# A fused attention and long-convolution kernel: 24 places of the stored task order are changed

## The chip, the cores and the metric

One core of a Trainium2 chip runs the kernel. The metric is the device time of one execution in microseconds; lower is better. The core's engines work in parallel and each takes its own queue in order: TensorE (PE, matmuls, with its weight loads PEld), VectorE (DVE), ScalarE (ACT), GpSimd (POOL) and SyncE (SP). SP and POOL mostly issue DMA transfers here.

## The reference

There are 8 batches of 3136 rows, 256 columns wide, and two parts that follow each other. The first is an attention without softmax, the second a gated long convolution through the Fourier transform.

```python
scores = (1 / S) * z @ z.T                    # z: 3136 x 64
out    = maximum(scores, 0)**2 @ v            # v: 3136 x 256
x      = u * out
x1, x2, x3 = split(x @ w_proj, 3)             # each 3136 x 256
conv   = irfft(rfft(x2, axis=rows) * rfft(filter, axis=rows))
result = (x1 * conv * x3) @ w_out
```

## The kernel before

**Tiles.** The 3136 rows of a batch are cut into 25 row tiles of up to 128 and, the other way, into 7 chunks of 512, 512, 512, 512, 512, 256 and 320 columns of the score matrix. A *unit* (b, c, k) is the k-th small group of row tiles (two, mostly) of chunk c in batch b.

**A unit's steps.** TensorE makes the scores into a PSUM pair (task kind S). A *relu* copies them into a buffer R (on ACT at line 1956 or on DVE at line 1958), and a *square* writes the bf16 weights into a buffer A (ACT at line 1965, DVE at line 1967). TensorE then multiplies A with v in two halves, called W and V, into the chunk's accumulator. There are 8 buffers A, 3 buffers R and 4 PSUM pairs; scores, accumulators and all later matmuls share the pairs.

**Mirrors.** The score matrix is symmetric. For the next two chunks a unit is not computed again: a DMA transpose on SP's queue (line 1885) writes the transposed A into a *mirror tile*, M_t for the next chunk and M2e_t or M2o_t for the one after, and the units of kind M read it. There is one buffer of each, so a new mirror can be written only when the last reader of the old one is done, and an A buffer that is mirrored comes free only when its transposes have landed.

**After the last unit of a chunk.** DVE multiplies the accumulator with the transposed u (line 2012); two projections and a product (line 1293) make the gates x1·x3; another projection and a first transform (`dft1`) go to a scratch in DRAM, from which the spectrum's matmuls (kind Q, products at line 1394) load it. The result goes to DRAM again, and for each chunk an inverse transform, a product with the gates (line 1499), the output matmul, an eviction to `ost_t` (two buffers) and a store (line 1548) follow. This tail of one batch runs between the units of the next. Inputs are cast on the way in by POOL's DMAs: z (line 662, then a copy that doubles it on DVE, line 1650, and a transpose on SP, line 1657), v (line 688), u (line 662, then a transpose on SP, line 1602). A small copy on POOL (a *tick*, lines 673 and 676) makes such a cast wait for a unit.

**The order.** `Plan.go` does not plan: it reads a stored list. `ORDER` holds two characters for each task, of all engines in one sequence; each task is emitted in that sequence, and so each engine's queue is the subsequence of its own tasks. `ENGINES` says for each of 1426 tasks that could run on either whether ACT or DVE does it. `BANKS` gives the number of the PSUM pair to each of 1054 tasks that take one. A few entries of `ORDER` are *fillers*, matmuls whose result nobody reads.

```python
for k in codes:
    if k >= len(every):
        self.fill(k - len(every))
        continue
    task = every[k]
    ...
    self.run(task, e, start)
```

SP waits inside its queue: a transfer that is not ready holds all behind it. Its DMA issues use eight semaphores in turn.

Of the kernel before, what the change touches and what calls it, by code (L numbers as in the profile page):

```python
# [20 lines left out]
NJ = 16  # L21
# [34 lines left out]
    "r}r~2e3Y2f363ks03i3Z3l2g2u372h2w3as13r3B3ss23vs33w2p3b2i2q3c3m2js42k3t3d3n3e3x3f3C2l0c2v0es50d3Q3y3R"
    "s60f3$0g3D3%3)s73j3*s83&3q3Ss93+3;3p3u3<3#3o3(3z3:3=3!3E3,sA3F494G4AsB3>4H3/0lsCsD4B4I0msE0nsF4N4J4C"
    "4K4OsG0o4R4D3-4S3?4E3G4TsH4P444X4UsI4Y3H3T4F3I4b3U454L4csJ4M4Z4i4W4d4msK4n4j0p4e4V3.0q4Q0r4o4a4f4vsL"
    "4k0s4h4p3J4wsM4l4g4x3K3@3L3V4q4?sN464ssO4@3[sP3]50sQ4t514u4[4y520t57473^4]584^sR0usS0v533_4z4_4{594|"
    "0w4}5D4r3{5M4:5EsT4;4~5NsUsV5FsW565O5h555A5l5i5s5B5C5msX5G545JsY5t5wsZ5j5L5#3M5n5P5x5K3N5usa5o5$sb5y"  # L60
# [2046 lines left out]
```

## Time and profile before

| what | value |
|---|---|
| median of three runs | 946.8 us (941.12, 946.80, 946.83) |
| profiled execution: device time, span | 942.77 us, 940.9 us |
| busy: PE, DVE, ACT, POOL | 97%, 89%, 87%, 26% of the span |
| mean granted TensorE clock | 0.997 |
| moved by DMA | 170.70 MB, 181 GB/s in the mean |

The page gives busy times by engine, the span in 40 slices, the DMA queues, the chain of work that ended last, and groups of instructions by line. Beside it the trace answers for a stretch: busy time by engine, or the instructions in order of time. A line of the latter gives start and length in us, engine, line, operation, output <- input, a count, and in brackets the engine's idle time before it with what ended it. "SPq" is SP's queue; the length of a DMA issue there is that of the issue, not of the transfer.

### The profile page before, as it was taken

The page shows a single profiled execution, that of the slowest core. Times are in us where ns is not written, and L with a number is a line of the kernel's source. Part 1 is how long each engine was busy: PE and PEld are TensorE (multiplying, and loading weights), DVE is VectorE, ACT ScalarE, POOL GpSimd, SP SyncE. Part 2 cuts the span into 40 slices and gives each one's busy share as a digit, 9 for nine tenths or more (in the row PEclk, how much of TensorE's full clock was granted, in tenths as well). Part 3 has the DMA queues.
Part 4 walks back from the last instruction along what each step waited for, and adds up shares of the span by engine and source line. Part 5 has one row for each costly group of instructions (what it writes and reads, how often), then busy time and mean ns, then how long its engine had stood idle before and what let it go on. Part 6 is the DMA issues. An engine that isn't in the chain of part 4 may idle for free.

```text
span 940.9 us, 30306 instructions
## 1 busy us (share of the span) xinstructions
PE 914.0 (97%) x12425; PEld 555.4 (59%) x12425; DVE 838.7 (89%) x1117; ACT 819.6 (87%) x952; POOL 247.6 (26%) x585
## 2 busy tenths in 40 slices
PE   8999999999999999999999999999999999999985
PEld 3445655566554666556565565666565666676654
DVE  8886899999888998999889988999988999899795
ACT  7877898999889998898989999899988999899673
POOL 5143322332332312223122231333123141101030
PEclk9999999999999999999999999999999999999999
DMA  9899899989999789998999989998999979898867
GB/s 158 155 176 163 141 156 197 185 144 173 169 218 201 151 190 168 206 200 146 192 173 212 177 160 189 178 223 149 200 167 208 224 128 202 202 205 140 207 193 232
DMA packets 331644, 170.70 MB, mean 181 GB/s; under 512 B 242887, under 2 KB 307143, under 8 KB 331505
## 3 DMA queue, kind: packets, MB, share of 16 engines
q1 hardware_dynamic: 301624, 131.98, 70.2%
q0 software_dynamic: 29168, 35.13, 25.8%
q8 instruction: 97, 1.59, 0.7%
q10 hardware_dynamic: 712, 1.66, 0.6%
q14 instruction: 43, 0.34, 0.2%
HBM read 90.26 MB, written 53.05 MB: 152 GB/s over the span
## 4 chain that ended last, share of the span: by engine, by line
PE 83%; ACT 5%; DMA 5%; DVE 5%; issue 2%; SPq 0%; POOL 0%; DVEq 0%; ACTq 0%; POOLq 0%
PE ps_s L553 82%; DMA M_t<-A_t 3%; ACT R_t L1956 2%; DVE xh L1394 1%; DVE A_t L1967 1%; DMA zn_t<-in_z_dram 1%; ACT A_t L1965 1%; DVE xT_t L2012 1%; DMA A_t<-spec 0%; ACT xh L619 0%; DMA spec<-uT_t 0%; ACT ost_t L619 0%; ACT s_t L619 0%; DVE gs_t L623 0%; ACT R_t L619 0%
## 5 line engine op out<-in xcount | busy, mean ns | idle before, releaser
L553 PE MATMUL ps_s<-A_t,v_t 64*128 64x512 bf16 (+5 forms) x4766 | 515.7, 352 | 1.1 <-DVE A_t L1967 1.0
L553 PEld LDWEIGHTS <-v_t 64*128 64x128 bf16 (+1 forms) x6528 | 305.8, 98 | 185.9 <-PE ps_s L553 19.2
L1956 ACT ACTIVATE R_t<-ps_s 128x1024 f32<-128x1024 f32 (+3 forms) x359 | 336.8, 961 | 50.4 <-PE ps_s L553 47.2
L1965 ACT ACTIVATE A_t<-R_t 128x1024 bf16<-128x1024 f32 (+2 forms) x281 | 271.8, 992 | 12.0 <-DVE R_t L1958 4.9
L1967 DVE SCALAR_TENSOR_TENSOR A_t<-R_t 128x1024 bf16<-128x1024 f32 (+3 forms) x211 | 233.6, 1123 | 17.6 <-ACT R_t L1956 10.3
L553 PE MATMUL ps_s<-zT_t 64*128 64x512 bf16 (+5 forms) x1186 | 191.4, 352 | 4.4 <-DVE gate_t L1293 1.7
L1958 DVE TENSOR_SCALAR R_t<-ps_s 128x1024 f32<-128x1024 f32 (+4 forms) x153 | 170.3, 1124 | 23.7 <-PE ps_s L553 13.3
L676 POOL COPY tick<-A_t 1x1 bf16<-1x1 bf16 x159 | 54.3, 341 | 426.0 <-ACT A_t L1965 262.0
L553 PE MATMUL ps_s<-xT_t,wp 64*128 64x512 bf16 (+3 forms) x976 | 124.3, 352 | 0.5 <-DVE R_t L1958 0.4
L553 PEld LDWEIGHTS <-zT_t 64*128 64x128 bf16 (+1 forms) x1219 | 68.9, 97 | 52.8 <-issue 9.8
L553 PE MATMUL ps_s<-M_t,v_t 64*128 64x512 bf16 (+4 forms) x860 | 96.6, 353 | 1.8 <-DMA M_t<-A_t 1.7
L619 ACT ACTIVATE x_t<-ps_s 128x1024 bf16<-128x1024 f32 (+3 forms) x75 | 69.4, 927 | 20.9 <-PE ps_s L553 18.1
L1394 DVE TENSOR_TENSOR xh<-xh,H 128x1024 bf16<-128x1024 bf16 x120 | 81.8, 685 | 2.9 <-ACT xh L619 2.0
L1293 DVE TENSOR_TENSOR gate_t<-ps_s,x_t 128x512 bf16<-128x512 f32 (+2 forms) x112 | 64.5, 617 | 12.4 <-PE ps_s L553 10.3
L2012 DVE TENSOR_TENSOR xT_t<-ps_s,uT_t 128x512 bf16<-128x512 f32 (+2 forms) x112 | 64.0, 614 | 6.5 <-PE ps_s L553 6.1
L1499 DVE TENSOR_TENSOR yT_t<-ps_s,gate_t 128x1024 bf16<-128x1024 f32 (+2 forms) x53 | 56.9, 1078 | 12.9 <-PE ps_s L553 11.7
L553 PEld LDWEIGHTS <-wp 64*128 64x128 bf16 (+1 forms) x976 | 47.8, 96 | 30.0 <-PE ps_s L553 2.0
L553 PE MATMUL ps_s<-wp,xT_t 64*128 64x256 bf16 (+2 forms) x944 | 64.0, 266 | 0.1
L553 PE MATMUL ps_s<-wo,yT_t 64*128 64x256 bf16 (+2 forms) x904 | 62.3, 266 | 1.0 <-DVE yT_t L1499 0.5
L662 POOL DMA_DIRECT2D un_t<-in_u_dram x112 | 58.1, 519 | 18.5 <-issue 16.0
L688 POOL DMA_DIRECT2D v_t<-in_v_dram x112 | 58.4, 525 | 13.6 <-issue 10.3
L553 PEld LDWEIGHTS <-xT_t 64*128 64x128 bf16 (+1 forms) x944 | 43.5, 97 | 19.1 <-issue 0.6
(157 smaller groups left out, 910.2 us busy)
## 6 DMA issues: line engine op xcount, KB each, us to landing
out_dram<-ost_t SPq DMA_DIRECT2D x60, 256.0 KB
spec_in_t<-spec SPq DMA_DIRECT2D x56, 192.0 KB
spec<-gs_t SPq DMA_DIRECT2D x56, 192.0 KB
v_t<-in_v_dram POOLq DMA_DIRECT2D x80, 128.0 KB, 4.5
un_t<-in_u_dram POOLq DMA_DIRECT2D x80, 128.0 KB, 4.5
spec<-s_t SPq DMA_DIRECT2D x40, 256.0 KB
conv_in_t<-spec SPq DMA_DIRECT2D x34, 256.0 KB
out_dram<-ost_t SPq DMA_DIRECT2D x18, 128.0 KB
```

Source lines behind the costliest of these rows:

```text
L553: got = nc.tensor.matmul(o, *args, **kw)
L619: got = nc.scalar.activation(out_, in_, AF.Copy)
L662: nc.gpsimd.dma_start(out=t[ds(j * N1, N1), lo - t0 : hi - t0, :], in_=x[:, n2 : n2 + hi - lo, :])
L688: nc.gpsimd.dma_start(out=t[ds(j * N1, N1), ds(v_at(a), (b - a) * D)], in_=r[:, n2 + a - lo : n2 + b - lo, :].rearrange("p t d -> p (t d)"),)
L1293: has_read(nc.vector.tensor_tensor(o[:, :, ::-1] if h == 0 else o, p, x, ALU.mult), p)
L1394: nc.vector.tensor_tensor(x[:, 1 - i], x[:, 0], h, ALU.mult)
L1499: has_read(nc.vector.tensor_tensor(yb["y"][:, :, 0:w], p, gates[b, c][:, :, 0:w], ALU.mult), p)
L1956: has_read(nc.scalar.activation(r, p, AF.Relu), p)
L1958: has_read(nc.vector.tensor_single_scalar(r, p, 0.0, ALU.max), p)
L1965: nc.scalar.activation(a, r, AF.Square, scale=1.0 / float(S))
L1967: nc.vector.scalar_tensor_tensor(a, r, inv_s2, r, ALU.mult, ALU.mult)
L2012: has_read(nc.vector.tensor_tensor(x[:, :, ::-1] if h == 0 else x, f, ut, ALU.mult), f)
```

## The change

No task is added or taken away but one filler (14 in place of 13), and no code changes: the three strings are others. Written out, 462 of some 5,480 tasks stand at another place against the rest of the list, but most of these only trade places with tasks of other engines. On its own engine's queue the order changes for 33 tasks, in these places:

| engine | what moves |
|---|---|
| PE | chunk (0,1): V(0,1,0) goes ahead of score (0,1,9) and the first gate projection of chunk (0,0), and that projection ahead of that score |
| PE | W(0,3,5) three and W(0,3,6) two places back, so that V(0,3,3) and V(0,3,4) come sooner; V(0,3,5) two places back, behind two scores |
| PE | V(0,4,5) two places forward; two of the filter's first transforms three places back |
| PE | V(2,3,2) ahead of W(2,3,5); V(4,2,4) forward and W(4,2,8) back by three; V(5,2,3) and V(5,2,4) three forward, W(5,2,5) four back |
| PE | score (5,4,6) and a projection of chunk (5,1) change places, with two tasks between them |
| PE | among the last tiles a gate projection goes ahead of an output matmul and the inverse transform behind it |
| ACT, DVE | relu (0,1,7) and square (5,3,6) go from DVE to ACT; squares (3,2,8) and (3,2,9) change places; the z copy of line 1650 at 621 us goes behind the eviction that follows it |
| SP | five output stores go back by 4, 8, 7, 6 and 5 places (before, at 281, 300, 395, 541 and 618 us); behind the first come a spectrum load and three mirror transposes, behind the fourth three mirror transposes, two writes of a spectrum and a transpose of u; a spectrum write at 306 us goes back by three |
| SP | transposes of u at 166 and 485 us go back by two and three; a mirror transpose at 274 us goes ahead of a spectrum load; one of the last batch's spectrum loads goes back by three, behind loads for the output of the batch before |
| POOL | at 64 to 70 us a z cast and a v cast go ahead of a tick and the last filter load; a tick at 307 us goes back by four |

`BANKS` follows from the order: 25 tasks take a PSUM pair that another task held before them than was the case. The diff is long; these are its first rows, the rows of the two letters of `ENGINES`, and the first row of `BANKS`:

```diff
 ORDER = (
     "0G0H00010203130I170J1404050K1806150L190716080C1B091G0D1Crx1H0A1A0B1D1L1I1Q0E1M0O1F0F1K1R1N1V1Zry1Wrz"
-    "1S1P1a1c110M1Xr!1d1U1g0N1b1Er#1h1k1Y1er$1l1o1J1ir%1f1p1m1s1j1=1tr&1qr(1>1]1n1u1}1^22r)231r1?1v271_r*"
+    "1S1P1a1c110M1Xr!1d1U1g1E0N1br#1h1k1Y1er$1l1o1ir%1f1J1p1m1s1j1=1tr&1qr(1>1]1n1u1}1^22r)231r1?1v271_r*"
...
 ENGINES = (
-    "aadddddddaaddaaaaaaddaaaddaadaadaadadadadaaaadadaddadddaaaadaadaaddaadaadaaddaddaaaaaaaaadadaddaddad"
+    "aadddddddaaddaaaaaaddaaaddaadaadaadadadadaaaadadaddadddaaaadaadaadaaadaadaaddaddaaaaaaaaadadaddaddad"
...
-    "aaaaaddadaadadadadaaaaddaaadadaaddadadaaaadadaaddadadaaaaaaaddadadaaaddaaddaaaaaadaaaadaaaaaaadadaad"
+    "aaaaaddadaadadadadaaaaddaaadadaaddadadaaaadadaaddadadaaaaaaaddadaaaaaddaaddaaaaaadaaaadaaaaaaadadaad"
...
 BANKS = (
-    "0123012312313213213213212301303103030132132132132321231210210102102123213123121323101201201202303203"
+    "0123012312313213213213212330130130303102102102102021201213213132132120210120121021232032032030131031"
```

More of the change, by code (lines that the diff above doesn't have):

```diff
@@ L56 @@
[L56 to L60, printed above, removed]
@@ new lines @@
+    "r}r~2e3Y2f363ks03i3Z3l2g2u372h2w3as13r3B3ss23vs33w2p3b2i2q3c3m2js42k3t3d3n3e3x3f3C2l0c2v0es50d3Q3Ss6"
+    "0f3$0g3D3%3)s73os83*3ys93&3R3;3p3j3<3q3+3u3#3!3=3(3:3z3E3,493F4G4AsAsB3/4H3>0lsC4B4IsD0msE0nsF4J4K4N"
+    "4C4O0osG4R3-4D4S3?4E3G4TsH4P444X4UsI4Y3H3T4F3I4b3U454L4csJ4M4Z4W4i4d4msK4n4j0p4e4V3.0q4Q0r4o4a4f4vsL"
+    "4k0ssM4p4h4w4g3J4l4x3K3@4s3L3V4q4?sN46sO4@3[sP3]4t50sQ514u4[4y52573^584]sR474^0t0usS530v3_4z4_4{594|"
+    "0w4}5D3{4r5M4:5EsT4;4~5NsUsV5FsW565O5h555A5l5i5s5B5C5m5GsX545JsY5t5wsZ5j5L5#3M5n5K5P5x3N5usa5o5$sb5y"
@@ new lines @@
+    "5H3O5k5)5q5*sc5Q5-3P5%5r5.3|4<5e5&5v5f4=5+3}5(5z3~5<sd485=5I4!se5/5!5>4#sf4$5?5^5p0x0y5,5_5@0z5}sg5:"
+    "5;5{5~5]0!7n7r607osh7vsi7ssjsk7w4%7psl5|5[7t4&7x7z61404(7!sm41sn427%627q7&7u7#437k7)7lso7*7.7(4)7y7/"
+    "7$7?7+4*7@sp4>4+7_7,7-7{7:5R7~5Ssq5T7[sr7;7<807>7|847]0#ss85815U0$5V7^5W0%88827}86st898D8a0&su8E8b83"
+    "7=8f8Asv8F878c8m8Bsw8n8C8g8Gsx8o0(8q8h8d0)sy0*8e8r8i0+sz8j0,8xs!8H8ys#8#8k8s8$8V8l8W0;4,638zs$4-648t"
+    "4.8p8%8u8+s%654/8:8w8,8&8;8v5X8(s&5Y8-665Z5g8[s(8)8<8]8!8|s)8}8^8=9K8*9L8>8/8~9S8.679T8@0-689Ms*0.0/"
@@ new lines @@
+    "8_0<s+0=s,0:5a8{5b8I8X5c0>909U0?5d690@8J9V9Y8K6A9Zs-7m9Ws.0{9N6B9a9O9b91s/8Y9c9P9i9Q9j9F9d9n8?9Gs:9t"
+    "9o9R9u9y9k9e9X9f8L9ps;9z6C8M9v9h9q8N9r6D0[6Es<9w9m9!0]9)A1s=9*A29s9#9$6F0^s>9+0_0|9xs?9g0}0~8O109(A3"
+    "9l8P928Q8ZAB9Hs@A46GA59,ACAF93AGs[AD6TAMs]94s^AH8RANs_9I8SA69-8TAIAQs{A7AR9{958U9|98AOAS9&96A8AX97A9"
+    "AJAY9%99ATs|AU9AAb9J6HAcAA6I9.AZs}AjAE6JAk6M9/6K6jAL6N6LA)AP9:A*s~6RAd6Ot09BAl6SA:AKAe9CAWAft1A;6P6U"
+    "AVt26Q6VAa9Dt3A+Ah6ZA[t46W6at59}9;6XA]Ai6b6c6Y9<6dAm9=6ht6A<t76eA,6iA=A{AnA>A-6zA|A.A^6k6fB2A#A/A$6g"
@@ new lines @@
+    "B69E6lt89~B7t9B36pA?6m6qA@AgA}tAB4BD6nA~9>B06otBBE6r9?B8tCA09@BHA_BFB9BIBQBAB5tDBRB1BJBCBlBvBGA%BmBB"
+    "BwBK6sBLBP6t6x9[A&6ytEBS9]tF6u9^BNB!AoB#tGBntH9_BT6vBxB)BOApBo6wtIB*BqAqB$tJBMB<tKBrB=BUBsB%BtB&C8tL"
+    "C9tM6!B>BiB+BuBj6#BzB,B(CAB-CCtNCJCD6$6(BytO6)CKB;Ar6%tPB/CE6+As6&6,tQCFBpAtAuCLCNtRB:AvCO6-6:AwB?6."
+    "CB6*tS6;6/CSCHtTB@CT6<CPCICUC5B.A(Ax6=CVCXCWAyCYCMAztUC6CbCQ6>CZCgCRChCnCctVCoCaBVCiA!CdCrtWCpEECsCj"
+    "BWCkCeEFBXtXCGBYCfCtEIEGBZEJtYEMCmBaENCqCu6?BbEK6}tZEOtaBcEQClBkB[BdtbERtcB]tdB^teESEUEXEVEHELCvEPEY"
@@ new lines @@
+    "Gut+Fx7NGSt,GTGDGv7OG&GJG(GCGO7PFyGwt-GZG+Fz7cG)GxG<GyC,GWF!t.G=Gat/G,G>GV7QG@7RF-G[t:C^7SGzG-t;F#Gb"
+    "G]G}G.G!G/F.F$G~G^G#GpF/G_G$F%GqGcH0H2GdH3t<GUGeC-G%C.H4t=7LHAC<HBt>C/G*DAH5t?C=C:H6HXC;t@HYC_C>G;C{"
+    "G?C?HeC[H8C@HCt[C]G|HfD0G:t]C|H1D1D3Grt^G{D4C}HlF&C~t_Hm7VF(D57T7WH9F)7XGfHDD6HZ7YD7HpGgHgHnD2t{7Zt|"
+    "HqHht}GhHi7aHaHrHvt~HEHwHsDQHzHbHcH!HxHSGiHTF*HFH#GsH)GjHdH*GtH$HGH%H7u0GkHHH-u1HtH.D8H+HjD9H@HkH[Hu"
+    "DBH/Hou2DCICH]DGH=H:u3H;u4DHIDu5DJH&HyDKDD7dH(HUDEIE7eHVH,7fGlIMu6INDFGmIRH?GnDLu7ISH^IOGou8IXIHH<DM"
@@ new lines @@
+    "ufD$L)LaL*ugD<L-IrL#uhL.DqLxIsL$LyLbL%ItL&I!L>IuuiL+L?LpL]LqIvL(IwL/ujL^JNIxL,M0L@L:JOL_ukDvJPulM1L{"
+    "L;DwL<M5L|umDxM6L=MCunM2MDJQJTM7JRL}L[JSJUD%M8JVK)MEM9M3MHL~MID&LrM4MFD(MJD+JWMBMGMKLsD,JXLcD-JYuoLd"
+    "D_LfLeJZupLgMeDyLhuqMfMmurusMnutD)D=MgMLLiD>MhMoLjMAD?MZMsMaMiMtMjLkMvMkMwE3LtMpMMMuMqM$MNJaM%LlMxuu"
+    "uvMOM*LmuwMyM+JnLnMluxM,M:D.M;M&uyM-M?M.M!MrM<M}M@M#MzM)M~M(D/M[NLD:M/NVuzMbNMM]M>NWu!N0NZu#NNNgMPNa"
+    "M=u$NXMQNONhM^u%LoNPD@MRNbM{JbD[JcNcM|D]MSD;u&NiJdJgN1MTJeJhu(J%JfMdNQMUJoN2u)JpNRNkM_Jiu*NGNlNHNrJq"
@@ new lines @@
+    "JlJjNSNsMcMVJkNTNdNUNtJmJtMWu+JuJru,NvJsMXu-NYNmNeNwJwJ#NfJxNjJ$NnNoN%u.N&JvNqNxN3J&u/JyJ(NyNzN}N(Np"
+    "N4N~NuJzu:N5O5J!N$O6OCJ@J)u;D{O0N)ODu<OGO7J*D|u=MYD}O1N#OHu>O8J+O9OMN6N*ONO2D^N7OEu?NIN]u@N8N^OIJ,NJ"
+    "OQJ-O3OOD~O4OJORE0N!OAOKE1J/OBOSJ:E4J>J.u[J?E5J;J[OTu]OUE6J]u^OXOLJ<u_OYK0J=OFK1J^ObOVOkOcu{OZOPN9J_"
+    "OlE2O(OWJ{NAO)K2u|NKO<u}OdNBN+OaOmK3OhOeOjOfNCK4O=N,OnN_OiO*N-O-u~NDv0O+O>N{NEO[v1O.O]O/OoN.v2v3NFO:"
+    "O^O}O$v4OgO%P7O~N/P8O;P0O_PSO{v5N:PTO@P1PWO?O|P9v6PUE7PXP4PdP6E8PeN;PYv7P5PfE9PhPAPZO,N<PiPmv8EAN=N|"
@@ new lines @@
+    "TNKiKXS;T8TFT9S9KwKjTATLT0TGT1SAQ1vlTOSBTTTYTBSKTHTZKfTCTUTPvmvnTaTISCS<TVSDTbTSS%TcSETeTQS=TfvoS>vp"
+    "TjTgS?TkSFTXS@TRTrTlS[T;vqTdTsTmTiT<TnTWvrTtTqT2T{U0Q2T|U1vsT=vtQ3KkT}TuT>QET?KlQ4Q7KmvuQ8vvThKpU7vw"
+    "Q5U8KqT@TvT[U9QUUBvxKrT,T]UCT-Q6S]T^Q9S^UDTpU2vyT4T_S_UEUIUFQAUMvzUJT3U3QBS{U4T~UNS|UKQCv!S}QFv#QGTo"
+    "QDU6UUv$UVQKQHKnTwUAQLQIKsTxQJS~UOKtQNTyUHU5KuULUPUQUWv%QOUrv&UsT.UyUGQSQPUTUzKxv(QQQTUXQRKyTzUtKzQV"
+    "QMT!v)QWT#U(v*U)v+QkQXT$U!QaUYT%UuQbT:U#UvQYU$T/UZT&QZUmUwUnQdUaU*QeUSv,UbUxU,QfU<URU-v-QgU@U=U%QhU&"
@@ new lines @@
+    "YRQ)Q@YawHVSQ/YTYWYdQ*YeQ:YbQ+YXwIQ;Q,YYYiwJQ~YjYfYmV+Q-wKYnV,YkYcYhYgYoYrV-Y;wLY<YswMYlY@Y=YqYtY}Yp"
+    "Q<wNY[Q=YuY~Q>YSV.wOY]V/Z2V:V[wPZ0Y>Z3Y^Q?Y_Y?Y{YvZ9Y|ZAQ[wQZ4Q]Y,ZDZBY-R7V;wRV<Q^wSZEwTZ5Z1V=Z6Z7ZF"
+    "Z8ZKZCZLWhV>ZGWnZHWiZIWoZMWjWkwUWpWlZPWmX}ZJZQwVZWYwZXZRZbZNZOZcwWY.ZSZTQ_ZYYxY/Q{ZyYyQ|wXZZwYZVZzZd"
+    "Z)WqwZZ*Q}WrZ/WsZaZ!ZeZ+Z#WtZ:Z<Z$waZ=Z,Z;Z%Z-wbZUZ>wcZfZ&Z^wdZ?Z_Z~ZtZ(Zua0wea5Z{aAa6YzZ@wfa1aBwgY!"
+    "Z[R0aCa2Y#Z.a3Z]aIZ|Z}aDa7aJR1afaEwhR2a4aKa8a9apagaHaqatwiaLauaha!aGR3wjara#aiR4ajR8wkRFR5ZvwlR9a&av"
@@ new lines @@
+    "RARNwmaka(WuwnawalaMa$Y$a.woW*a/Y%aaabwpY&ama)Zwa<ana=a_Y(aoa{aFa:Y)bIwqY*a|Zgwra>bJY:axZhwsa*a+ZiY+"
+    "bPasbQa?ayZja@bKZmZkazZlbWwtbXZna,WvZoZxbRa%wuWwacbSW!bTa-W#RBWxadwvbaWya;bbWzRCW_W+W$RDZpa^W,Zqa}Zr"
+    "bga]wwW%W(bhW&aNwxbYW)bLR6aObiW-bMbNbcaPa[W:wyW.bdwzW;beW/W=w!a~W>bOZsbkw#REblW?W]bDbUbEaQW^W@RGbVW<"
+    "W[bmRHaRRIW{w$aSW|bnbZbobrw%XBbsW}bvX1w&W~bww(X0b&btbfbjX2bqb(X4bubxRJX5w)bpb|RKb)w*b}bybzX9w+X3RLX6"
+    "w,XAb~c7b%cCb*c8b#c2X7c0c3cDw-X8cIw.b$cJbFw/w:b+c9c4c5cRaTcEb!cKw;b^cmb_w<cSaUcncFcLc6aeaVcAcBcTcHcq"
@@ L156 @@
[L156 to L160 removed]
+    "Xacffqcgfzfuf&chXbd8f+f#f:Xdcid9f;Xef,dAxIf-XsxJXff?dEf@f(dFf<xKdGf|f!dBf}f/dCXgf[dDerg2f.Xhg3f~f>f]"
@@ new lines @@
+    "f^XlxLXifcgPf=xMg4f{XmgXgQX!xNgYxOfdxPXng1gZgddHxQgRgeg0gadIfNgbg5dJfOgfXodKfPxRXpxSf_XqgSg6gggTghgU"
+    "XjgngKxTgLgogsXtgVXrgtXuxUXvX#gixVX+gygpgWgzgjgkX$xWguX=fQX%gcdLg%gvfRgwg!g&fTxXgmfSg(glg.fUg/grg)fV"
+    "fexYg*gqh6gxh7XwfWg$g:fXh8g-XxgMfYg7h9hAxZXyg8dYhGxag9hHxbhKg#g;hLhIhRgAxchSfZgBgNhVhMgCxdgDhWxehNhT"
+    "hOgEg,dMgFgOg<hBhCdNg+hchDhdh1hXdRh2xfhEdSdOgGdZgHXzhYdPdaxghZdQhghFgIdodThJhQdbhhxhdUhohexidVg=h/hp"
+    "dcgJxjddhUh:hPhiX&g>hqh@X(g?hahjh[xkhkxlh;X)hbX,dWh]h3hmX-xmX.h}dXhfh^h~h_hndeh4g@dfhri2g[i0hli3xng]"
@@ new lines @@
+    "i8dhi9xodgxpi4xqdidmi5hsh<i6dnd&h=iCh>iAdjh)iJh*dpiKh?X*iDh{h|dqdkX/xrdlX:iEdxdrg^xsX;dyiFxtiGiLX<g_"
+    "dsiNg{h5dudtxui7i1dvdziWiBiOiXiId$dwxvd!d%xwd#iMiriPd(iHisxxxyd-iYd)iQiViTiRxzd.h+i#X>d*iZh,itx!i$i)"
+    "X?x#i*d+iug|x$X@i%g}iUhtiaiwg~hux%ixhvd,i/h0ioi]x&ipiyi:iSizi+i!i^hwi;jEi,hxi-jFx(i<x)hyi_jIi(i&i.iv"
+    "jJi[jGjPd:hzjQi?d;i{jKh!jRx*i@h.d<h#jTjLi=d?x+jUx,d@d=x-jYjdx.d>jZjeh$jHi|h%jVjNh&jOjBjajhjmjCjSjijW"
+    "jXjfjnh(jtjbibjcd/jjjujxx/joicjyjgidk{jpx:jvjMjkl0i>k|x;jzx<d[h-l1jqjll4x=d]k}x>jsiel5d^l8x?l9jwl2x@"
@@ L161 @@
+    "qRqhrlqaqjqiqbrqqkrrqoqcqdqlqqqprsqmqnrmmVqsrtqrmWrnrumYmXk;mZrvk<may?mky<y?y<k=y?n#n&n$qtk>n%q%n(k?"
+    "q:n=n)q_k@y>r5y<y>y<rFy>k[quo]rPqvqwy=q&o^q(o_o{q)q;qxq<qyq=q*qzo|q+q!p6o}q>q,q$q#r6pvq-r7q?r8q/q.py"
+    "q@pwpzq[pxrwr9q]q^rGrAp!rHrBrIq{rCrQq|rRrDrEq}rJrSrKq~rLrMrTr0rUrOr2r1rWrVr4rNrXr3"
 )
 ENGINES = (
-    "aadddddddaaddaaaaaaddaaaddaadaadaadadadadaaaadadaddadddaaaadaadaaddaadaadaaddaddaaaaaaaaadadaddaddad"
+    "aadddddddaaddaaaaaaddaaaddaadaadaadadadadaaaadadaddadddaaaadaadaadaaadaadaaddaddaaaaaaaaadadaddaddad"
```

153 lines of the change are left out of this document (47 added, 106 removed).

## The prediction

> **What bounds the kernel now.** I read the page first, then the busy time by stretches, and then the idle times of TensorE one by one. The page:
>
> ```profile
> span 940.9 us, 30306 instructions
> PE 914.0 (97%) x12425; PEld 555.4 (59%) x12425; DVE 838.7 (89%) x1117; ACT 819.6 (87%) x952; POOL 247.6 (26%) x585
> PE 83%; ACT 5%; DMA 5%; DVE 5%; issue 2%; SPq 0%; POOL 0%; DVEq 0%; ACTq 0%; POOLq 0%
> ```
>
> TensorE is busy for 914.0 of 940.9 us and carries 83% of the chain that ended last. No matmul is removed or added but one filler, so a new order can only win what is idle: 26.9 us. The stretches (columns: length, busy PE, weight loads, DVE, ACT, POOL, granted clock, DMA share, GB/s) say where that lies:
>
> ```profile
> 50.00:280.00 230.00, 228.64 (x2900) 130.44 (x2898) 203.00 (x254) 200.99 (x228) 70.97 (x165) 1.00 1.02 172
> 280.00:300.00 20.00, 18.32 (x245) 9.69 (x235) 16.62 (x27) 18.34 (x22) 6.10 (x14) 1.00 1.11 216
> 300.00:540.00 240.00, 236.80 (x3314) 146.52 (x3310) 219.36 (x289) 217.25 (x248) 61.48 (x149) 1.00 1.00 182
> 540.00:560.00 20.00, 19.35 (x288) 13.49 (x285) 17.98 (x24) 17.96 (x25) 6.58 (x17) 1.00 0.92 159
> 560.00:850.00 290.00, 289.43 (x4022) 185.26 (x4020) 266.02 (x341) 266.06 (x299) 67.00 (x160) 1.00 0.99 189
> ```
>
> From 50 to 850 us TensorE is idle for 1.36 + 1.68 + 3.20 + 0.65 + 0.57 = 7.46 us. The other 19.4 us lie before 50 and behind 850, where the change has one place at the start and a few at the end. Also 560 to 850, with 0.57 us in 290, holds several of the changed places; nothing can be won there. So the ceiling of the whole change is about 7.5 us plus a little at the ends, 0.8% and some.
>
> **The largest term: the store that goes behind three mirror transposes.** Around 293 us TensorE has one of its longest idle times.
>
> ```profile
> 280.95 2.28 SPq L1548 DMA_DIRECT2D out_dram<-ost_t  x2
> ...
> 287.90 2.65 SPq L1885 DMA_TRANSPOSE M_t<-A_t  x2
> ```
> ```profile
> 290.64 0.42 DVE L1399 TENSOR_TENSOR xh<-xh 128x512 bf16<-128x512 bf16 x1
> 292.84 1.23 DVE L1967 SCALAR_TENSOR_TENSOR A_t<-R_t 128x1024 bf16<-128x1024 f32 x1 [1.78 <-ACT ost_t L619]
> 293.98 1.28 DVE L1293 TENSOR_TENSOR gate_t<-ps_s,x_t 128x512 bf16<-128x512 f32 x2
> ```
> ```profile
> 295.31 0.39 PE L553 MATMUL ps_s<-zT_t 64*128 64x512 bf16 x2 [1.69 <-DVE gate_t L1293]
> ```
>
> Read from the end. The score matmul at 295.31 waits 1.69 us for the PSUM pair that the gate product (L1293) reads. That product waits behind the square at 292.84, and VectorE stood idle for 1.78 us before the square. The named releaser, an output copy on ScalarE, gives the square nothing: it needs its own relu and a free A buffer, and A buffers are released when their transpose into a mirror tile has landed. The first transpose of the pair at 287.90 reads such a buffer, so I take its landing, at about 292.8, to be what ended the wait; this is inferred, not named by the view. In the new order the store at 280.95, two issues and 2.28 us of SP's queue, goes behind a spectrum load and three transposes, the two at 287.90 among them. Their squares and the last readers of their mirror tile stand several units earlier in the order, so I take them to be ready and held by the queue alone: they move forward by 2.28 us, the square's 1.78 us of idle time goes, and with it the score's 1.69 us. What is late next is the work right behind the score, which waits for nothing in this trace. Term: −1.69 us, with bounds 0 and −1.69. The store itself has one more output tile to spare in its two-buffer pool; if that cover were gone it would cost at most its own 2.28 us of queue.
>
> Here the DMA share is 1.11 in the row 280 to 300 above: the engines that move the bytes are full too. The Trainium skill, "DMA: Bandwidth & Descriptors", section "Issuing engines are not separate DMA queues", says that transfers issued from Scalar, Sync and GpSimd all run on the same 16 DMA engines and interleave. By that rule an earlier issue need not mean an earlier landing, and this term would be 0 in place of −1.69; it is the first rival below.
>
> **The same edit at 541 us.** A store (two issues, 1.18 us) goes behind three transposes, an input transpose and two spectrum writes.
>
> ```profile
> 541.09 1.18 SPq L1548 DMA_DIRECT2D out_dram<-ost_t  x2
> 542.37 6.08 SPq L1885 DMA_TRANSPOSE M_t<-A_t  x3
> ```
> ```profile
> 549.09 0.47 ACT L1965 ACTIVATE A_t<-R_t 128x320 bf16<-128x320 f32 x1 [0.94 <-DMA M_t<-A_t]
> ...
> 551.05 1.37 ACT L1965 ACTIVATE A_t<-R_t 128x640 bf16<-128x640 f32 x2 [0.31 <-DMA M_t<-A_t]
> ```
> ```profile
> 550.20 0.39 PE L553 MATMUL ps_s<-x_t,T 64*128 64x512 bf16 x2 [0.49 <-ACT R_t L1956]
> ...
> 553.06 0.39 PE L553 MATMUL ps_s<-zT_t 64*128 64x512 bf16 x2 [0.16 <-ACT R_t L1956]
> ```
>
> Here the view names the DMA: ScalarE's squares wait 0.94 and 0.31 us for the landing of a transpose, and TensorE then waits 0.49 and 0.16 us for the relus behind them. The transposes come 542.37 − 541.09 = 1.28 us sooner, more than 0.94. Term: −0.65 us, bounds 0 and −0.65.
>
> **The mirror at 80 us.** Two weighing halves that read the old mirror tile (V of units (0,3,3) and (0,3,4)) go ahead of W of (0,3,5) and (0,3,6).
>
> ```profile
> 66.98 0.59 PE L553 MATMUL ps_s<-M_t,v_t 64*128 64x512 bf16 x4
> ...
> 67.84 0.60 PE L553 MATMUL ps_s<-M_t,v_t 64*128 64x512 bf16 x4
> ...
> 79.92 0.60 PE L553 MATMUL ps_s<-M_t,v_t 64*128 64x512 bf16 x4 [0.91 <-DMA M_t<-A_t]
> ```
> ```profile
> 68.52 4.31 SPq L1885 DMA_TRANSPOSE M_t<-A_t  x2
> ```
>
> The matmuls at 67.84 are the last readers of the mirror tile; they end at 68.44, and SP's transposes start at 68.52. In the new order they take the place of those at 66.98, 0.86 us sooner. TensorE later waits 0.91 us for the second of these transposes, so the term is −0.86 us; the bounds are 0 and −0.91, since the casts that POOL moves forward at the same place share the DMA engines. On POOL a z cast and a v cast pass a tick and a filter load; the load's first reader is one of the filter's last transforms, dozens of tasks on, so it is priced at 0.
>
> **The start.** Relu (0,1,7) goes from VectorE to ScalarE and three matmul groups change places.
>
> ```profile
> 29.25 0.76 PE L553 MATMUL ps_s<-zT_t 64*128 64x512 bf16 x4 [1.12 <-DVE xT_t L2012]
> 30.38 0.61 PE L553 MATMUL ps_s<-xT_t,wp 64*128 64x512 bf16 x4 [0.37 <-DVE R_t L1958]
> ```
> ```profile
> 27.91 1.28 DVE L2012 TENSOR_TENSOR xT_t<-ps_s,uT_t 128x512 bf16<-128x512 f32 x2
> 29.11 1.22 DVE L1958 TENSOR_SCALAR R_t<-ps_s 128x1024 f32<-128x1024 f32 x1
> ```
> ```profile
> 28.54 1.02 ACT L1956 ACTIVATE R_t<-ps_s 128x1024 f32<-128x1024 f32 x1
> ```
>
> Before, the score waited for the product that ended at 29.19 and the projection for the relu that ended at 30.33. Now the score (0,1,8) takes the pair that this relu frees. On ScalarE the relu takes the place at 28.54 and ends at about 29.56, so the score starts at 29.60, 0.35 us later than now. Behind it stand a weighing half (0.43 us a group of four: 66.98 and 67.84 are two groups apart), the projection, the other score and the projection's second half, none of which waits: 29.60 + 0.22 + 0.43 + 0.43 + 0.22 = 30.90, where it starts now at 30.38 + 2 × 0.43 = 31.24. Term: −0.34 us. Against it stands 1.02 us more for ScalarE: relu (0,1,6) and the squares of (0,1,4) and (0,1,7) queue behind the new relu, and if TensorE waits for one of them up to 1.02 comes back. Bounds −0.34 and +0.68; I take −0.34, as by the order four weighing groups that need none of these stand first.
>
> **The end, and what is priced at nothing.**
>
> ```profile
> 928.59 0.61 PE L553 MATMUL ps_s<-wo,yT_t 64*128 64x256 bf16 x8 [0.29 <-DVE yT_t L1499]
> ```
>
> Among the last tiles a projection goes ahead of an output group, and the group that feeds the product before 928.59 starts about 0.2 us sooner: −0.2, bounds 0 and −0.29. The other three stores moved back, the squares (3,2,8) and (3,2,9) that change places, the square (5,3,6) that goes to ScalarE, the z copy, and the weighing halves in batches 2, 4 and 5 lie where TensorE waits for none of their kind: batch 5's places lie in 560 to 850, with its 0.57 us of idle time. Their cover is a TensorE queue that is full; without it each would be worth its own instruction, about a microsecond. The loads put a few places later have their consumers many tasks behind them. All these get 0; the bounds are −0.65 (the smaller of the two stores' terms, once more) and +1.02 (one more relu in ScalarE's queue).
>
> **The sum:** −1.69 − 0.65 − 0.86 − 0.34 − 0.2 = −3.74 us. Against the profiled execution's own 942.77 us (its span of 940.9 and 1.9 around it) that is 939.0; against the median of 946.8 it is 943.1. The runs shown are 941.12, 946.80 and 946.83, and with the profiled one their mean is 944.4; less 3.7 it gives 940.7, and I forecast 941 us. 5.7 us of scatter between runs is more than the term itself. One per cent is 9.5 us, about what a measurement of this kernel can tell from no change.
>
> **The rivals.** *The landings do not move, or the list changes less than it seems* (0.35). Most differing characters of the list are tasks of different engines that trade places between each other, which alters no queue; 33 tasks change their order on their own engine. And the DMA share of 1.11 at the main place says that the transposes may land when bytes get through, not when they are issued. For it: that share. Against it: at 541 the share of the stretch is 0.92, and there the named wait is a landing. Only 0 to 1 us is then won (the start and the end): 943.4 to 944.4 from the mean, 941 to 947 by the runs. The skill's rule above speaks for this one.
>
> *Slower: the stores come back* (0.10). Five stores now stand later in SP's queue, among a spectrum's writes and loads. If each blocks SP there and a load behind it becomes what TensorE waits for, the price is their issue time: 2.28 us for the one shown, 1.18 for the other, and the three others, of two issues each, lie between those: 7.0 to 10.3 us in all with no gain. I take 7.0, since the stretch of the larger has the higher DMA share: 942.77 + 7.0 = 949.8 from the profile, 953.8 from the median. It decides from the point where the loads behind a store have less than its 1.18 to 2.28 us to spare. Against it: stores leave the queue's place that the transposes wait for, and nothing in the trace waits for an output store. Only beyond 956.3 is it over 1%: 0.03.
>
> **How the numbers follow.** Forecast 0.55, with its own range 941.12 − 3.74 = 937.4 to 946.83 − 3.74 = 943.1; no gain 0.35; slower 0.10. The range 936.5 to 947.5 holds the first two by the scatter of the runs, and leaves out most of the third and the tails. Faster by over 1% means below 937.3, which needs the whole sum and the fast end of the scatter: 0.09. Slower by over 1%: 0.03. Within: 0.88.
>
> **What would show it.** In the new profile VectorE's idle time before the square near 291 us should be under 0.3 us and the score's 1.69 us gone; ScalarE should not wait for a DMA near 548; the mirror's wait near 79 should be about 0.1 us; near 29 the gate projection should start before the second score. TensorE's idle time from 50 to 850 should be about 4.3 us where it is 7.46. If it is still 7 us or the idle time has only moved on to another place, the second case holds. If TensorE waits for spectrum or conv loads that it did not wait for, the third.

## The result and the profile after

The changed kernel takes 950.94 us in the median of 14 runs (947.14 to 955.90), the kernel before 942.62 us (14 runs, 936.90 to 950.74). The ratio is 1.0077, with a 95% interval of 1.0052 to 1.0102: slower by 0.8%, where 941 us and a small gain were forecast. The ratios here and below leave disturbed runs out, the medians do not. The profiled execution took 955.24 us, 12.5 more than that of before.

The page of the changed kernel, the lines that answer to those of before:

```profile
span 953.5 us, 30308 instructions
PE 918.9 (96%) x12427; PEld 556.0 (58%) x12427; DVE 837.0 (88%) x1115; ACT 819.9 (86%) x954; POOL 246.7 (26%) x585
PE 77%; DMA 9%; DVE 6%; ACT 5%; issue 2%; SPq 0%; DVEq 0%; POOL 0%; ACTq 0%; POOLq 0%
```

TensorE is busy 4.9 us longer with the same matmuls (and one filler more), and idle 7.7 us longer: 34.6 in place of 26.9. DMA has gone from 5% to 9% of the chain. The busy time by stretches of the changed kernel (columns as in the prediction) says where:

```profile
50.00:78.00 28.00, 28.00 (x274) 13.15 (x270) 23.44 (x35) 18.13 (x21) 9.14 (x23) 1.00 1.17 153
78.00:94.00 16.00, 11.32 (x89) 4.70 (x87) 6.86 (x9) 8.03 (x9) 4.15 (x10) 0.79 1.26 168
94.00:280.00 186.00, 185.57 (x2462) 109.20 (x2460) 167.00 (x206) 166.95 (x191) 53.97 (x126) 1.00 0.98 164
280.00:292.00 12.00, 9.31 (x110) 4.95 (x108) 6.72 (x8) 8.81 (x10) 3.72 (x10) 0.86 1.11 192
```

Two stretches stand out, 78 to 94 and 280 to 292. Both have idle time, and in both the granted clock is below 1. The same first stretch before had 155 matmuls where there are now 89:

```profile
78.00:94.00 16.00, 15.00 (x155) 8.79 (x153) 9.97 (x13) 12.89 (x14) 6.56 (x14) 1.00 1.22 171
```

**Near 79 us.** TensorE's order of time in the changed kernel:

```profile
83.16 1.03 PE L553 MATMUL ps_s<-M_t,v_t 64*128 64x512 bf16 x4 [4.58 <-DMA M_t<-A_t]
...
84.42 1.06 PE L553 MATMUL ps_s<-A_t,v_t 64*128 64x512 bf16 x4
...
92.42 0.59 PE L553 MATMUL ps_s<-A_t,v_t 64*128 64x512 bf16 x4
```
```profile
80.50:83.20 2.70, 0.04 (x2) 0.04 (x4) 0.00 (x0) 0.63 (x1) 1.57 (x4) 0.76 1.30 123
83.20:88.00 4.80, 4.80 (x24) 1.71 (x26) 1.23 (x1) 2.43 (x3) 0.77 (x3) 0.50 1.21 165
```

The first row is the group that started at 79.92 us before, after 0.91 us of waiting for its mirror tile. It now waits 4.58 us, and then the clock is halved: a group of four takes 1.06 us in place of 0.59. Matched task by task, TensorE was 0.43 us ahead of before when it came to this place; the waiting group starts 3.2 us late, and at 94 us TensorE is 6.2 us late. So the longer wait costs 3.7 us, and the halved clock behind it nearly all of the other 3. From there to 274 us the distance stays at 6.2 us.

**Near 281 us** come another 4 us, 10.4 in all at 292: a square waits for a mirror's landing, TensorE waits for the relu behind it, and the clock halves again.

```profile
281.77 1.06 ACT L1965 ACTIVATE A_t<-R_t 128x1024 bf16<-128x1024 f32 x1 [3.48 <-DMA M_t<-A_t]
```
```profile
283.79 1.04 PE L553 MATMUL ps_s<-wp,xT_t 64*128 64x256 bf16 x8 [2.69 <-ACT R_t L1956]
```

From 50 to 850 us TensorE is idle for 13.5 us, where 4.3 had been forecast. A smaller loss of 3 us lies between 640 and 750 us, where the prediction saw nothing to win; no experiment was made for it.

**At the first place the diff touches POOL and TensorE**, 12 to 16 us earlier. POOL's queue before and, in the second fence, after:

```profile
64.88 1.23 POOL L762 DMA_DIRECT2D xh<-in_moe_filter_fft_dram  x2 [0.29 <-issue]
...
67.64 1.58 POOL L662 DMA_DIRECT2D zn_t<-in_z_dram  x3
69.17 0.57 POOL L688 DMA_DIRECT2D v_t<-in_v_dram  x1
```
```profile
64.43 1.55 POOL L662 DMA_DIRECT2D zn_t<-in_z_dram  x3 [0.73 <-issue]
65.94 0.56 POOL L688 DMA_DIRECT2D v_t<-in_v_dram  x1
...
66.57 1.23 POOL L762 DMA_DIRECT2D xh<-in_moe_filter_fft_dram  x2
```

The filter load is issued 1.7 us later. The mirror transposes (68.52 us and 4.31 us for the two before) are issued sooner, and their issues hold SP's queue for much longer:

```profile
67.22 7.44 SPq L1885 DMA_TRANSPOSE M_t<-A_t  x2
74.72 3.85 SPq L1885 DMA_TRANSPOSE M2o_t<-A_t  x1
```

The view of the DMA issues gives, as its last number, the time from issue to landing of the two large transfers of the filter load, before and after:

```profile
xh<-in_moe_filter_fft_dram POOLq DMA_DIRECT2D x2, 256.0 KB, 5.6
```
```profile
xh<-in_moe_filter_fft_dram POOLq DMA_DIRECT2D x2, 256.0 KB, 8.5
```

By these rows load and transposes now stand in each other's way. That is the theory which the experiments start from.

### The profile page after: what moved, and what is told of

The parts are those of the page before. It is cut to its first block, busy times and chain, and to the rows that moved or that the text cites. A ratio compares the mean times of both kernels' runs of the same rounds, so it can differ in the third digit from the quotient of the medians.

```text
span 953.5 us, 30308 instructions
## 1 busy us (share of the span) xinstructions
PE 918.9 (96%) x12427; PEld 556.0 (58%) x12427; DVE 837.0 (88%) x1115; ACT 819.9 (86%) x954; POOL 246.7 (26%) x585
## 4 chain that ended last, share of the span: by engine, by line
PE 77%; DMA 9%; DVE 6%; ACT 5%; issue 2%; SPq 0%; DVEq 0%; POOL 0%; ACTq 0%; POOLq 0%
PE ps_s L553 77%; DMA M_t<-A_t 5%; ACT R_t L1956 2%; DVE xh L1394 1%; DMA M2e_t<-A_t 1%; DVE A_t L1967 1%; DMA spec<-gs_t 1%; ACT A_t L1965 1%; DMA v_t<-spec 1%; DMA A_t<-spec 1%; DVE xT_t L2012 1%; ACT xh L619 1%; DMA spec<-s_t 0%; DVE yT_t L1499 0%; DVE xh L1399 0%
## 5 line engine op out<-in xcount | busy, mean ns | idle before, releaser
L1956 ACT ACTIVATE R_t<-ps_s 128x1024 f32<-128x1024 f32 (+4 forms) x360 | 337.3, 962 | 50.2 <-PE ps_s L553 42.5
L1965 ACT ACTIVATE A_t<-R_t 128x1024 bf16<-128x1024 f32 (+3 forms) x282 | 272.7, 993 | 20.6 <-DMA M_t<-A_t 11.0
L1967 DVE SCALAR_TENSOR_TENSOR A_t<-R_t 128x1024 bf16<-128x1024 f32 (+4 forms) x210 | 232.4, 1123 | 25.4 <-ACT R_t L1956 11.3
L1958 DVE TENSOR_SCALAR R_t<-ps_s 128x1024 f32<-128x1024 f32 (+2 forms) x152 | 169.0, 1123 | 25.3 <-PE ps_s L553 15.4
```

The costliest lines, as they stand in the source:

```text
L1956: has_read(nc.scalar.activation(r, p, AF.Relu), p)
L1958: has_read(nc.vector.tensor_single_scalar(r, p, 0.0, ALU.max), p)
L1965: nc.scalar.activation(a, r, AF.Square, scale=1.0 / float(S))
L1967: nc.vector.scalar_tensor_tensor(a, r, inv_s2, r, ALU.mult, ALU.mult)
```

## The experiments

The experiments were timed beside the kernel before on the same chip, in five rounds. "Wait" is TensorE's wait for the mirror near 79 us in the one profiled execution of each; before, it is 0.91 us.

| kernel | median, us | ratio to before, 95% interval | wait, us |
|---|---|---|---|
| changed | 950.94 | 1.0077 [1.0052, 1.0102] | 4.58 |
| changed, stretch at 64 us as before | 944.26 | 1.0014 [0.9982, 1.0046] | 0.15 |
| before, with that stretch as changed | 949.53 | 1.0061 [1.0033, 1.0090] | 2.88 |
| before, POOL's part of it alone | 950.30 | 1.0044 [1.0008, 1.0079] | 2.29 |
| before, TensorE's part of it alone | 946.90 | 1.0032 [0.9998, 1.0066] | 1.67 |
| changed, filter load late | 951.33 | 1.0075 [1.0039, 1.0112] | none; 2.55 at 93 |
| before, casts ahead and load late | 952.96 | 1.0095 [1.0058, 1.0133] | none; 9.37 at 93 |
| before, load early | 944.44 | 1.0001 [0.9965, 1.0036] | none |
| changed, load early | 947.92 | 1.0031 [0.9995, 1.0066] | none |
| changed, 14 fillers ahead of the wait | 951.27 | 1.0102 [1.0068, 1.0136] | 1.48 |
| before, SP's places alone | 942.95 | 1.0005 [0.9969, 1.0040] | none |
| before, other places of PE, ACT and DVE | 944.31 | 0.9995 [0.9961, 1.0029] | none |

### Is it the stretch at 64 us?

Diffs of the list are written as the order of tasks on a queue. The changed kernel, put back there:

```diff
 POOL
-z cast, v cast, tick (0,3,8), filter load
+tick (0,3,8), filter load, z cast, v cast
 PE
-V(0,3,2) V(0,3,3) V(0,3,4) S(0,3,11) W(0,3,5) W(0,3,6) W(0,3,7)
+V(0,3,2) W(0,3,5) V(0,3,3) W(0,3,6) V(0,3,4) S(0,3,11) W(0,3,7)
```

> The changed kernel with one stretch of the list put back to the order of before: the one near 64 to 70 us, which holds POOL's two casts and the weighing halves V and W of chunk (0,3). Everything else is as changed. Theory A (this stretch makes TensorE wait 4.58 us near 79 us and run at a granted clock of 0.50 for about 7 us after it): the wait goes back to about 0.9 us, the clock stays at 1.00 from 78 to 90, and the time falls by about 6 us from the 950.9 of the changed kernel, to 944 to 946, within 0.4% of before. Theory C (the wait is an accident of the one profiled execution, and the 8 us are spread over the other places): no fall, 950 to 952, 0.8% over before.

The opposite edit on the kernel before:

> The kernel before with this one stretch alone changed (POOL's two casts ahead of the filter load, and V of (0,3,3) and (0,3,4) ahead of W of (0,3,5) and (0,3,6)). Theory A: TensorE waits about 4 us for a mirror near 79 us, the granted clock falls to 0.5 behind it, and the time is about 6 us (0.6%) over before, near 948.6. Theory C: within 1 us of before, near 942, the wait near 79 us 0.1 to 0.9 us.

Measured: 1.0014 without the stretch, 1.0061 with it alone. TensorE in the first of the two:

```profile
78.86 0.61 PE L553 MATMUL ps_s<-M_t,v_t 64*128 64x512 bf16 x4 [0.15 <-DMA M_t<-A_t]
```

Theory A holds in both directions, theory C falls. Some 0.6 of the 0.77% are this stretch. Two things did not come as expected: the second kernel waits 2.88 us and not about 4, and behind that wait the clock stayed at 1.00.

### POOL's part or TensorE's?

Each part of the diff above was put alone into the kernel before.

> The kernel before with only POOL's queue changed in this stretch: the z cast and the v cast go ahead of the tick and the filter load; TensorE's order is that of before. Theory A1 (the later filter load is what the mirror transposes meet on the DMA engines): wait near 79 us of 3 to 5 us, 5 to 6 us (0.6%) over before. Theory A2 (it is TensorE's order, which lets the transposes be issued 1.3 us sooner, into the casts): no change, within 1 us of before. Theory A3 (only the two together do it): no change either, so the next kernel decides between A2 and A3.

> The kernel before with only TensorE's order changed in this stretch: V of (0,3,3) and (0,3,4) ahead of W of (0,3,5) and (0,3,6); POOL's queue is that of before. Theory A1: the mirror's wait near 79 us falls from 0.91 us to about 0.1 us, as the prediction's term has it, and the time is 0 to 0.9 us under before. Theory A2: wait of 3 to 5 us, 5 to 6 us over before. Theory A3: no change.

POOL alone: 1.0044, a wait of 2.29 us and a halved clock behind it (three rows of the stretches, then TensorE's row):

```profile
82.00:83.00 1.00, 1.00 (x8) 0.41 (x6) 0.68 (x1) 0.71 (x1) 0.00 (x0) 0.61 1.10 201
83.00:84.00 1.00, 1.00 (x8) 0.33 (x6) 0.00 (x0) 0.97 (x2) 0.00 (x0) 0.50 1.13 290
84.00:85.00 1.00, 1.00 (x8) 0.45 (x6) 0.00 (x0) 0.40 (x1) 0.20 (x2) 0.50 1.31 244
```
```profile
81.38 0.60 PE L553 MATMUL ps_s<-M_t,v_t 64*128 64x512 bf16 x4 [2.29 <-DMA M_t<-A_t]
```

TensorE alone: 1.0032, with an interval that touches no change. Its transposes are issued at 67.34 us, 1.2 us sooner than before, and the wait is 1.67 us, longer and not 0.1 us as the prediction had it. No theory was right alone: A1 saw POOL's part, with a wait shorter than it said, but its gain from TensorE's order did not come. Which part is the larger the two times cannot tell, as their intervals overlap. Both edits push transposes and load into one another, one by a later load, one by earlier transposes.

### Is it the load? Two other places for it

Late first, behind eight tasks of POOL's queue (the expectation counts 12), in the changed kernel and then in the kernel before with the casts ahead:

```diff
 POOL
-... filter load, u cast, tick, tick, v casts, u cast, tick, tick, z cast
+... u cast, tick, tick, v casts, u cast, tick, tick, z cast, filter load
```

> The changed kernel with one task moved: the last filter load on POOL (four transfers, two of 256 KB) goes 12 places back in POOL's queue, behind the z cast near 80 us, so that it is issued when the mirror transposes of 67 to 75 us have landed; its first reader stands near 106 us. Theory A (load and transposes share the DMA engines, and the transposes land late by that): the 4.58 us wait near 79 us falls under 0.5 us, the clock stays at 1.00 there, and the time falls by 6 us or more from 950.9, to 942 to 945. Theory D (the casts or the earlier issue of the transposes do it, not the load): the wait stays over 2 us and the time over 948.

> The kernel before with only POOL's queue changed: the two casts go ahead as in the kernel where POOL alone was changed (0.44% over before), but the filter load goes behind the z cast near 80 us. Theory A: the wait near 79 us is under 0.5 us (0.91 us before, 2.29 us with POOL's queue changed as in the diff), and the time is 0 to 0.9 us under before. Theory D: the wait stays over 2 us and the time 0.4% over before.

The wait at 79 us is gone in both, and the two mirror transposes, at 67.20 and 68.41 us, issue in 2.65 and 2.66 us. The two casts are still issued as early (64 to 66 us), so it is not they alone that delay the mirror. But the time has not moved (1.0075 and 1.0095). SP and TensorE in the first of the two:

```profile
67.20 2.65 SPq L1885 DMA_TRANSPOSE M_t<-A_t  x2
...
84.26 3.61 SPq L1885 DMA_TRANSPOSE M_t<-A_t  x1
```
```profile
95.46 1.04 PE L553 MATMUL ps_s<-M_t,v_t 64*128 64x256 bf16 x8 [2.55 <-DMA M_t<-A_t]
```

and TensorE in the second:

```profile
102.37 1.03 PE L553 MATMUL ps_s<-M_t,v_t 64*128 64x256 bf16 x8 [9.37 <-DMA M_t<-A_t]
```

The load, issued at 80 to 83 us, meets the next mirror transposes at 84 us. The mechanism of theory A holds, its times do not: the load costs where it meets transposes, and here it met others. So a much earlier place was tried. This needs one edit of the code, since the load waits for the tick of chunk 2:

```diff
-filt_ld[c].deps = [(tick_, None)]
-tick_.kids.append(filt_ld[c])
+first = tick_ if c == 0 else first
+t = first if c == 2 else tick_
+filt_ld[c].deps = [(t, None)]
+t.kids.append(filt_ld[c])
```

> The kernel before with the last filter load alone moved forward, behind the two u casts near 31 us (it waits for the tick of chunk 0 in place of that of chunk 2, and stands some ten places earlier on POOL); a stretch from 42 to 45 us in which the DMA engines are nearly idle (share 0.06) lies behind it. Theory A (the load costs where it meets mirror transposes): no wait near 79 us (0.91 us before) nor near 93 us (2.55 and 9.37 us with the load put late), unless the load meets transposes of 30 to 42 us; time 0 to 2 us under before. Theory E (mirror transposes near 80 to 93 us are late anyway, whatever the load does): a wait of 2 us or more near 79 or 93 us, time 3 us or more over before.

> The changed kernel with the same move of the filter load. Theory A: the 4.58 us wait near 79 us is gone and none near 93 us takes its place; the time falls from 950.9 to 942 to 945. If the places outside that stretch are worth the 2.9 us that the prediction gave them, it goes under 941; if they are worth nothing, as the run without the stretch has it, it stays near 943. Theory E: 948 or more, with a wait near 79 or 93 us.

The waits near 79 and 93 us are gone in both. The changed kernel falls from 1.0077 to 1.0031, with intervals that still overlap; the kernel before stays where it was. Transposes at 67 us in the changed kernel:

```profile
67.32 2.90 SPq L1885 DMA_TRANSPOSE M_t<-A_t  x2
```

Theory E falls. But the new place is not free of transposes: those of the mirror near 35 us meet the load, and their issue is stretched. Before and, in the second fence, in the changed kernel with the load early:

```profile
35.84 2.62 SPq L1885 DMA_TRANSPOSE M_t<-A_t  x2
```
```profile
35.50 5.11 SPq L1885 DMA_TRANSPOSE M_t<-A_t  x2
```

TensorE is nevertheless busy for all of the 12 us from 34 to 46 us in both kernels. So the load costs where it meets transposes that TensorE soon waits for, and not with every transpose. The 947.92 us are above the 942 to 945 expected, but the interval reaches from 0.9995 to 1.0066 and holds 944; in this kernel's profiled execution the second loss is still there (a wait of 2.64 us at 276 us, with a halved clock). No version tried is measurably faster than the kernel before.

### What does the halved clock cost?

```diff
 PE
+14 fillers
 W(0,4,3)
```

> The changed kernel with 14 fillers (28 matmuls whose result nobody reads, about 3 us) on TensorE right ahead of the weighing half that waits 4.58 us near 79 us. The mirror lands when it lands; only TensorE is busy for most of the wait. If the clock is what the idle time costs beside its own length: idle time there falls to about 1.6 us, the granted clock stays at 1.00 from 80 to 90 us, and the time is 2 to 2.5 us under the changed kernel, 948.5 to 949. If the halved clock behind the wait costs nothing (other engines would have held TensorE): 951, as changed. Where the wait is shorter than 3 us in a run, the fillers cost the difference.

The clock stayed at 1.00 and the idle time at 1.48 us, as expected, and the time stayed at 951.27. TensorE, then ScalarE, then SP, in that kernel:

```profile
82.42 0.61 PE L554 MATMUL ps_s<-M_t,v_t 64*128 64x512 bf16 x4 [1.48 <-DMA M_t<-A_t]
91.04 0.61 PE L554 MATMUL ps_s<-A_t,v_t 64*128 64x512 bf16 x4 [1.92 <-ACT A_t L1966]
```
```profile
89.02 1.02 ACT L620 ACTIVATE s_t<-ps_s 128x1024 bf16<-128x1024 f32 x1 [2.66 <-DMA specf<-s_t]
```
```profile
77.99 0.57 SPq L1066 DMA_DIRECT2D specf<-s_t  x1
```

Against the changed kernel TensorE gained 2.7 us from 82 to 87 us, which is the clock, and gave 2.1 of it back at 89 us, where ScalarE waited for the landing of a spectrum write that was issued at 77.99 us, behind the transposes on SP's queue. So in this execution the halved clock was real, but most of it lay in the shadow of the same late landings.

### The other places

> The kernel before with SP's places alone: four of the five output stores, the spectrum write and loads, the transposes of u and the mirror near 274 us as changed (with the tick near 307 us, which goes with them); TensorE's order and the stretch at 64 us are those of before. By the prediction's two terms for the stores: 2.3 us under before, with the waits of 1.69 us near 294, 0.81 near 537 and 0.49 near 550 gone. By its rival (the stores come back): 5 to 8 us over before. By what the run without the stretch at 64 us suggests (all other places together 1.3 us over before, with a new wait of 1.5 us near 274): 0 to 2 us over before, the old waits gone and a wait near 274 in their place.

> The kernel before with the changed places of TensorE, ScalarE and VectorE outside the stretch at 64 us and outside SP's places (one store at 618 us goes with them). By the prediction: 0.34 us at the start and 0.2 us at the end are won, the others nothing: 942, within 1 us of before. If these places hold what the run without the stretch had over before: 944, with a wait of TensorE that is not in the trace of before near one of them.

Both are at no change. The prediction's 2.3 us for SP's places (0.9975) lie inside the first one's interval, so the size is not refuted; its rival of 5 us or more is. Near 294 us, with SP's places alone:

```profile
286.92 4.11 SPq L1885 DMA_TRANSPOSE M_t<-A_t  x2
```
```profile
293.37 1.23 DVE L1967 SCALAR_TENSOR_TENSOR A_t<-R_t 128x1024 bf16<-128x1024 f32 x1 [2.46 <-DMA M_t<-A_t]
```
```profile
295.85 0.39 PE L553 MATMUL ps_s<-zT_t 64*128 64x512 bf16 x2 [2.61 <-DVE gate_t L1293]
```

The transposes were issued 1 us sooner than before (287.90), their issue took 4.11 in place of 2.65 us, and the square came 0.5 us later. The wait that should have gone grew to 2.61 us.

The second loss of the profiled execution, near 281 us, is not tied to the diff: the same wait of TensorE for that relu is in the traces of the changed kernel and of four experiments (1.48 to 3.13 us), two of which have SP's and TensorE's orders of before, and in none of the other eight kernels. What makes it come and go was not settled.

## Why the prediction was wrong

- **The ceiling** was right as far as it went: an order can win only idle time. It was taken for the whole question. A new order can also make idle time, and that side had only the stores and about a microsecond for a relu in it.
- **"The load's first reader is dozens of tasks on, so it is priced at 0"** is the step that failed. Nobody waits for the load; but it shares the DMA engines with transfers that somebody waits for. POOL's edit alone measured +0.44%.
- **The mirror at 80 us, −0.86 us.** The transposes were issued 1.3 us sooner, as said; they landed 3 us later, and the term came out at about +6 us with clock and POOL's edit together. The prediction saw that the casts share the engines, and let this only cancel the gain: the bound ended at 0 where it had to reach above. Nor is the 0.91 us wait fixed: the two kernels of "The other places", which keep this stretch as before, do not have it.
- **The store at 281 us, −1.69 us.** The inference that the square waits for a landing is borne out: the row at 293.37, the same square in another kernel, names it. In the changed kernel the idle time is gone,

```profile
301.71 1.22 DVE L1967 SCALAR_TENSOR_TENSOR A_t<-R_t 128x1024 bf16<-128x1024 f32 x1
302.85 1.28 DVE L1293 TENSOR_TENSOR gate_t<-ps_s,x_t 128x512 bf16<-128x512 f32 x2
```
```profile
304.18 0.39 PE L553 MATMUL ps_s<-zT_t 64*128 64x512 bf16 x2
```

  and so it is in the three kernels made from the changed one by moving the load or adding fillers. In all six experiments that keep SP's order here TensorE's wait is still there, with 1.17 to 2.20 us. So the move of the store does reach this wait. But 0.72 us of it are left in the changed kernel without the stretch, and 2.61 us with SP's places alone. "They move forward by 2.28 us" took the issue's length for fixed and the landing for tied to it. Neither is.
- **The store at 541 us, −0.65 us.** In the changed kernel ScalarE no longer waits for a DMA there and TensorE's two waits are gone (the same squares, whose rows had 0.94 and 0.31 us before):

```profile
557.16 0.47 ACT L1965 ACTIVATE A_t<-R_t 128x320 bf16<-128x320 f32 x1
...
558.86 1.36 ACT L1965 ACTIVATE A_t<-R_t 128x640 bf16<-128x640 f32 x2
```

  That looks like a hit and is not one. The same waits are gone in all six experiments that keep this store at its old place; SP and ScalarE in the kernel with TensorE's order alone:

```profile
539.69 1.19 SPq L1548 DMA_DIRECT2D out_dram<-ost_t  x2
540.98 4.83 SPq L1885 DMA_TRANSPOSE M_t<-A_t  x3
```
```profile
547.32 0.46 ACT L1965 ACTIVATE A_t<-R_t 128x320 bf16<-128x320 f32 x1
```

  So these waits belonged to the one profiled execution of the kernel before, and no run shows that the edit wins anything here.
- **The start, −0.34 us:** right. The score waits 0.36 us longer, and the projection's second half starts at 30.81 us, 0.43 before its 31.24; 0.12 of that TensorE was ahead already. Across this place TensorE wins 0.31 us in all six kernels that have it changed, and 0.05 us at most in the other six.

```profile
29.49 0.39 PE L553 MATMUL ps_s<-zT_t 64*128 64x512 bf16 x2 [1.48 <-ACT R_t L1956]
...
30.81 0.60 PE L553 MATMUL ps_s<-xT_t,wp 64*128 64x512 bf16 x4
```

- **The end, −0.2 us,** cannot be read off as a time: TensorE goes from 11.6 us late at 908 us to 12.6 at the end. The wait of 0.29 us itself is gone in all six kernels that have this place changed, and is there in the six others.
- **The rivals.** The first, that an earlier issue need not land earlier, was the right mechanism. The rule cited for it from the Trainium skill ("DMA: Bandwidth & Descriptors", section "Issuing engines are not separate DMA queues") agrees with the rows at 286.92 and 67.22. But the rival was priced from nothing to 1 us of gain: transfers that interleave can also lose. The second rival put a loss at the stores, and SP's places alone (1.0005) show none.
- **Range and chances.** +0.77% is within 1%, which had 0.88, but by luck: what was forecast within 1% was a gain. The time is outside 936.5 to 947.5, since no case held a loss at the load.

## What to carry to other kernels

Price a moved DMA by what shares the engines with it while it is in flight, and not only by its own reader; where the mean DMA share is near 1, the bound of such a move goes above zero. A load put elsewhere can bring its cost along: look at what is queued for the next 10 us at the new place, and at who waits for it. A wait of under 1 us that one trace shows may not be there in the next execution: look for it in a second trace before a term is built on it. Where a matmul queue is full, a wait of about 2 us or more may have to be counted with the clock behind it, and then reduced by whatever is late anyway.

## What the runs showed of the hardware

**About 2 us of idle time can halve the clock, depending on where they fall.** Between 30 and 890 us the granted clock went to 0.50 behind TensorE's waits of 2.19, 2.20, 2.29, 2.55, 2.64, 2.69, 2.97, 4.58 and 9.37 us in these traces, and stayed at 1.00 behind others of 2.00, 2.61, 2.88 and 3.13 us. The records of the clock show why. In each trace it changes only on a grid with steps of 3.41 us; in the changed kernel at 81.88, 88.71, 283.27 and 286.68 us, for example. Counted by these steps, the nine steps at full clock with 2.02 us of idle time or more were each followed by a halved one, and none with 1.9 us or less was. Two steps of the kernel before with the load early (the 2.20 us wait), then three of the stretch at 64 us alone, where a border of the grid cuts the 2.88 us wait in two:

```profile
294.27:297.69 3.42, 1.40 (x13) 0.61 (x11) 2.31 (x3) 1.99 (x3) 0.78 (x3) 1.00 0.86 186
297.69:301.10 3.41, 3.22 (x20) 1.71 (x21) 2.46 (x4) 2.08 (x2) 1.91 (x5) 0.50 1.05 248
```
```profile
76.95:80.36 3.41, 1.51 (x15) 0.58 (x9) 2.85 (x5) 1.66 (x2) 2.02 (x4) 1.00 1.46 122
80.36:83.77 3.41, 2.42 (x24) 1.12 (x26) 1.23 (x1) 1.48 (x2) 0.01 (x1) 1.00 1.09 94
83.77:87.19 3.42, 3.33 (x34) 1.40 (x32) 2.32 (x2) 1.98 (x3) 1.74 (x4) 1.00 1.21 235
```

Behind 890 us, among the last tiles, steps with as little as 0.99 us of idle time were also followed by a halved one; why is open.

The Trainium skill, "TensorE: Matmul & The Clock Gate", section "What's actually happening", has the clock fall to half after an idle window of about 3.4 us that runs free of the kernel. These traces agree with a free-running window, by which 2.20 us can cost and 2.88 not; they differ in that about 2 us of idle time within a step were enough.

**The clock tells runs apart.** In the 14 runs of the changed kernel the mean granted clock goes from 0.995 in the fastest (947.14 us) to 0.987 in two of the slowest three (954.61 and 955.90 us). Part of the scatter of several us would thus come from how often a late landing led to a halved clock; only the profiled executions can show where it did.

**The issue of a transpose has no fixed length.** The same two mirror transposes near 68 us held SP's queue for 2.64 to 2.90 us in the four kernels with the filter load elsewhere, and for 3.19 to 7.44 us in the nine with the load in flight; all that stands behind them waits as long.
